# Reordered first loads and transposes in a squared-ReLU MLP kernel on one core

## The chip, the core and the metric

The kernel runs on one core of a Trainium2 chip. The metric is the time of one execution on the device in microseconds (us). TensorE (PE) does the matrix products and writes them to PSUM; VectorE (DVE) and ScalarE (ACT) move and transform data; GpSimd (POOL) and SyncE (SP) do little here but start transfers. DMA queues that SP, ACT and POOL issue to bring the inputs from HBM into SBUF.

## What is computed

`x` has 2048 rows of 576 numbers, `w1` is 576 x 4608, `w2` is 4608 x 576, all bf16:

```python
h = jnp.einsum("bsd,df->bsf", x, w1) + b1
r = jnp.where(h > zero, h, zero)
h = r * r
out = jnp.einsum("bsf,fd->bsd", h, w2) + b2
```

## The kernel before, in words

The 2048 rows are cut into four blocks of 512. A product with `w1` contracts over the 576 columns of `x`, so `x` must lie transposed in SBUF (`xTw`, one block per buffer, columns in windows of 128 partitions). For blocks 1 to 3 a transposing DMA does that (`load_xT`, L122). For block 0 it would come late, so PE does it: `x` is loaded as it is in four pieces of 128 rows (`x_sb`, `load_x` L71), and `x_transpose(j, k)` (L145) multiplies the 128 x 128 piece of row group j and column chunk k with an identity into a PSUM tile `tb`. I write T(j,k) for it. Chunks 0 to 3 are the first 512 columns; the fifth (k = NK) is the last 128, which overlap chunk 3 by half. Row groups 0 and 1 make half 0 of the block, 2 and 3 half 1. `x_copies(h)` (L151) then brings half h into `xTw` with five copies of 128 x 256: chunks 0, 2 and the fifth on DVE, 1 and 3 on ACT. Each of chunks 0 to 3 has a PSUM bank of its own for each half; the fifth shares the bank of chunk 2, in slot 1.

The 4608 columns of `w1` are 36 tiles of 128. The first four (`w1n`, and `w1n8` for the last 64 rows of the contraction) are the head of block 0: `a_full(0, "k_outer")` (L195) computes them while the rest of `w1` (`w1_h`) is still being loaded. Its unit is `part(h, k)` (L224): four matmuls of 256 columns, one per tile, that add chunk k of half h. The last 64 rows are added by `pair` (L202), four matmuls on 64 rows each that run two at a time. `dup_windows(0)` (L117) makes two big DVE copies within `xTw`, so that 64-row pieces lie in both halves of the partitions. `make_b1T` (L164) transposes the bias rows on PE into one bias per partition. After the head, `a_rows(0)` (L179) does the other 32 tiles with pairs of 64-row matmuls, and `evac_h` (L174) applies bias and ReLU on ACT and squares on DVE. The rest (`phase_t` and `phase_b`, the product with `w2`, and the three other blocks) follows on PE without a pause, in an order written out at L309 to L329.

The order of the head on PE before the change is: seven warm-up matmuls on constants (L61 to L63); T(0,0..3), T(1,0..3), the two fifth chunks, the copies of half 0; part(0,0); T(2,..); part(0,1), part(0,2); T(3,..), the copies of half 1, `dup_windows`; part(0,3), part(1,0), the bias transpose, part(1,1) to part(1,3), the pairs.

`keep` holds the instructions of each engine in the order of the program; the framework puts in the semaphore waits. It also gives every DMA that SP or ACT issues one of eight semaphores in turn, so that the ninth waits until the first has landed. SP issues x0, w1n0, w1n1, x3, w1n2, w1n3, then the first two pieces of `w1_h`, the two of `w1n8`, and the rest of `w1_h`; ACT issues x1 and x2; POOL issues `b1_rows` (36 rows of 256 B) and `b2_col` (L98, L100).

Of the kernel before, what the change touches and what calls it, by code (L numbers as in the profile page):

```python
# [11 lines left out]
BF16 = mybir.dt.bfloat16  # L12
FP32 = mybir.dt.float32
# [4 lines left out]
def kernel(  # L18
# [9 lines left out]
    nc = tc.nc  # L28
    keep = tc.keep_in_program_order
    P = 128  # L30
    H = 64
    x2 = x.flatten_outer_dims()
    out2 = out.flatten_outer_dims()
    S, D = x2.shape
    F = w1.shape[1]
    NFT = F // P
    NC = D // H
    NK = NC // 2
    G = 4
    GW = G * P  # L40
# [6 lines left out]
    DM = D - DT  # L47

    const = ctx.enter_context(tc.tile_pool(name="const", bufs=1))
    wpool = ctx.enter_context(tc.tile_pool(name="wpool", bufs=1))  # L50
# [5 lines left out]
    ps_h = ctx.enter_context(tc.tile_pool(name="ps_h", bufs=4, space=PSUM))  # L56
    ps_o = ctx.enter_context(tc.tile_pool(name="ps_o", bufs=4, space=PSUM))

    wps = ps_o.tile([P, 512], FP32, name="wps", tag="po")
    ones = nc.const_aps.tensor(1.0, [P, 512], BF16)  # L60
    WARM = [512] * 6 + [128]  # L61
    for i, n in enumerate(WARM):
        keep(nc.tensor.matmul(wps[:, 0:n], lhsT=ones[:, 0:P], rhs=ones[:, 0:n], start=True, stop=True))  # L63

    xs = const.tile([P, RT, D], BF16, name="x_sb")
    w1n = wpool.tile([P, NK, GW], BF16, name="w1n")
    w1n8 = wpool.tile([P, G // 2, P], BF16, name="w1n8")
    w1_h = wpool.tile([P, NC, FH], BF16, name="w1_h")
    w1_v = w1.rearrange("(c p) f -> p c f", p=H)

    def load_x(eng, rt):  # L71
        keep(eng.dma_start(out=xs[:, rt, :], in_=x2[rt * P:(rt + 1) * P, :]))

    def load_w1n(eng, k):
        keep(eng.dma_start(out=w1n[:, k, :], in_=w1[k * P:(k + 1) * P, 0:GW]))

    def load_w1n8(eng, h):
        src = w1[NK * P:D, 0:GW].rearrange("p (i h f) -> p i h f", h=2, f=P)
        keep(eng.dma_start(out=w1n8[h * H:(h + 1) * H, :, :], in_=src[:, :, h, :]))

    def load_w1(eng, h, j0, j1):
        keep(eng.dma_start(out=w1_h[h * H:(h + 1) * H, :, j0 * P:j1 * P],
                      in_=w1_v[:, :, GW + h * FH + j0 * P:GW + h * FH + j1 * P]))

    load_x(nc.sync, 0)
    load_x(nc.scalar, 1)
    load_w1n(nc.sync, 0)
    load_x(nc.scalar, 2)
    load_w1n(nc.sync, 1)
    load_x(nc.sync, 3)  # L90
    for k in range(2, NK):
        load_w1n(nc.sync, k)

    ident = const.tile([P, P], BF16, name="ident")
    make_identity(nc, ident[:])
    b1_rows = const.tile([P, P], BF16, name="b1_rows")
    nc.gpsimd.memset(b1_rows[:], 0.0)
    nc.gpsimd.dma_start(out=b1_rows[0:NFT, :], in_=b1.rearrange("(ft p) -> ft p", p=P))  # L98
    b2_col = const.tile([P, 1], BF16, name="b2_col")
    nc.gpsimd.dma_start(out=b2_col[:], in_=b2[DM:D].rearrange("(d o) -> d o", o=1))  # L100
    b2T = const.tile([P, 1], FP32, name="b2T")
    nc.gpsimd.tensor_copy(out=b2T[:], in_=b2_col[:])
    warm = const.tile([P, 1], FP32, name="warm")
    keep(nc.scalar.activation(out=warm[:], in_=nc.const_aps.tensor(0.0, [P, 1], FP32), func=ACT.Relu))

    E3, O, SPC, E = 0, 1, 5, 6
    LO_W = [O, O + 1, O + 2, O + 3, E, E + 1, E + 2, E3, SPC]
# [20 lines left out]

    w2_sb = wpool.tile([P, NFT, D], BF16, name="w2_sb")
    w2_view = w2.rearrange("(ft p) d -> p ft d", p=P)  # L130
    W2CH = 9

    def load_w2(c):
        keep(nc.sync.dma_start(out=w2_sb[:, c * W2CH:(c + 1) * W2CH, :], in_=w2_view[:, c * W2CH:(c + 1) * W2CH, :]))

# [2 lines left out]
    alloc_xT(0)  # L138
    xT0 = xT_blk[0]
    HS = SB // 2  # L140
    tb_po = [ps_o.tile([P, 2, HS], BF16, name="tb", tag="po") for _ in range(2)]
    tb_ph = [ps_h.tile([P, 2, HS], BF16, name="tb", tag="ph") for _ in range(4)]
    half_banks = [tb_ph, None]

    def x_transpose(j, k):  # L145
        h, q = divmod(j, 2)
        qc = slice(q * P, (q + 1) * P)
        bank, slot, c0 = (half_banks[h][k], 0, k * P) if k < NK else (half_banks[h][2], 1, D - P)
        keep(nc.tensor.transpose(bank[:, slot, qc], xs[:, j, c0:c0 + P], ident[:]))  # L149

    def x_copies(h):  # L151
        hc = slice(h * HS, (h + 1) * HS)
        for k in range(NK):
            src = half_banks[h][k][:, 0, :]
            if k % 2 == 0:
                keep(nc.vector.tensor_copy(out=xT0[:, O + k, hc], in_=src))  # L156
            else:
                keep(nc.scalar.copy(out=xT0[:, O + k, hc], in_=src))  # L158
        keep(nc.vector.tensor_copy(out=xT0[:, E3, hc], in_=half_banks[h][2][:, 1, :]))


    b1T = const.tile([P, NFT], FP32, name="b1T")

    def make_b1T():  # L164
        b1T_ps = ps_o.tile([P, P], BF16, name="b1T_ps", tag="po")
        keep(nc.tensor.transpose(b1T_ps[:], b1_rows[:], ident[:]))  # L166
        keep(nc.vector.tensor_copy(out=b1T[:], in_=b1T_ps[:, 0:NFT]))

# [26 lines left out]
    def a_full(sb, order):  # L195
        xT = xT_blk[sb]
        banks = []
        for g in range(G):
            pool, tag = (ps_o, "po") if g < 2 else (ps_h, "ph")
            banks.append(pool.tile([P, SB], FP32, name="pn", tag=tag))  # L200

        def pair(i, start, stop):  # L202
            keep(nc.tensor.matmul(banks[2 * i][:], lhsT=w1n8[0:H, i, :], rhs=xT[0:H, SPC, :],  # L203
                             start=start, stop=stop, skip_group_check=order == "k_outer"))
            keep(nc.tensor.matmul(banks[2 * i + 1][:], lhsT=w1n8[H:P, i, :], rhs=xT[H:P, E3, :],  # L205
                             start=start, stop=stop, skip_group_check=order == "k_outer"))

        def full(g, k, start, stop):
            keep(nc.tensor.matmul(banks[g][:], lhsT=w1n[:, k, g * P:(g + 1) * P], rhs=xT[:, O + k, :],  # L209
                             start=start, stop=stop))  # L210

        if order == "rows_first":
            for i in (1, 0):
                pair(i, True, False)
            for g in (2, 3, 0, 1):
                for k in range(NK):
                    full(g, k, False, k == NK - 1)
                evac_h(sb, banks[g], g)
        else:
            if order == "k_outer":  # L220
                tb_new = [ps_h.tile([P, 2, HS], BF16, name="tb", tag="ph") for _ in range(2)]
                half_banks[1] = tb_new + tb_po

                def part(h, k):  # L224
                    hc = slice(h * HS, (h + 1) * HS)
                    for g in range(G):
                        keep(nc.tensor.matmul(banks[g][:, hc], lhsT=w1n[:, k, g * P:(g + 1) * P],  # L227
                                              rhs=xT[:, O + k, hc], start=(h == 0 and k == 0), stop=False,
                                              skip_group_check=True))

                for j in range(2):
                    for k in range(NK):
                        x_transpose(j, k)
                for j in range(2):
                    x_transpose(j, NK)
                x_copies(0)
                part(0, 0)
                for k in range(NK + 1):
                    x_transpose(2, k)
                part(0, 1)  # L240
                part(0, 2)
                for k in range(NK + 1):
                    x_transpose(3, k)
                x_copies(1)
                dup_windows(0)
                part(0, 3)
                part(1, 0)
                make_b1T()
                for k in range(1, NK):
                    part(1, k)  # L250
            else:
                for g in (2, 3, 0, 1):
                    for k in range(NK):
                        full(g, k, k == 0, False)
            for i in (1, 0):
                pair(i, False, True)
                evac_h(sb, banks[2 * i], 2 * i)
                evac_h(sb, banks[2 * i + 1], 2 * i + 1)
# [35 lines left out]
    for (j0, j1) in [(0, 1), (1, 2), (2, 4), (4, 6), (6, 8), (8, 10), (10, 12)]:  # L294
        load_w1(nc.sync, 0, j0, j1)
        load_w1(nc.sync, 1, j0, j1)
        if j0 == 0:
            load_w1n8(nc.sync, 0)
            load_w1n8(nc.sync, 1)
    load_xT(1)  # L300
    for (j0, j1) in [(12, 14), (14, 16)]:
        load_w1(nc.sync, 0, j0, j1)
        load_w1(nc.sync, 1, j0, j1)
    keep(nc.sync.dma_start(out=b2_bc[:], in_=b2.partition_broadcast(P)))
    for c in (0, 2, 1, 3):
        load_w2(c)
    load_xT(2)

# [51 lines left out]
```

## Time and profile before

| | us |
|---|---|
| median of 5 runs | 290.97 (290.82 to 291.11) |
| the profiled execution, whole | 291.4 |
| its span, first to last instruction | 289.6 |
| PE busy | 285.6 (99%) |
| ACT busy | 96.7 (33%) |
| DVE busy | 78.5 (27%) |
| first transpose of x on PE begins | 3.65 |
| first `pair` on PE begins | 9.87 |

The profile lists instructions by the line of the program, with the engine, the tile that is written and those that are read, and the shape. In its timeline each row has the start and the length of a group in us, and in brackets how long the engine had been idle before it and what released it. A matmul's record reaches from its start to its modelled end and overlaps the next; the pace of PE is read from start to start. The profiled execution has its own time; a step is measured in it and then set against the median.

### The profile page before, as it was taken

How to read it: one execution, taken by the hardware profiler on the slowest of the kernel's cores; microseconds unless marked ns; L12 is line 12 of the kernel's file. 1: busy time of each engine (PE TensorE's matmuls, PEld its weight loads, DVE VectorE, ACT ScalarE, POOL GpSimd, SP SyncE). 2: the span in 40 equal slices, each digit the busy share in tenths (PEclk: the TensorE clock that was granted, in tenths of full speed). 3: DMA queues.
4: the chain of work that ended last, by engine and by line, in shares of the span. 5: the costliest groups of instructions: out<-in, count | busy, mean ns of one | idle time of the engine just before them, and what ended most of it. 6: DMA issues, size and time to landing. Idle time of an engine off the chain costs nothing.

```text
span 289.6 us, 4693 instructions
## 1 busy us (share of the span) xinstructions
PE 285.6 (99%) x2027; PEld 140.0 (48%) x2032; DVE 78.5 (27%) x176; ACT 96.7 (33%) x154; POOL 2.2 (1%) x10
## 2 busy tenths in 40 slices
PE   8999999999999999999999999999999999999996
PEld 5544444444444555555544444444444455555555
DVE  1644554444500200000015444444440001100001
ACT  2566666666500000000027666666670000000000
POOL 3000000000000000000000000000000000000000
PEclk9999999999999999999999999999999999999999
DMA  6999999800001200000000000000000110000100
GB/s 199 207 239 183 261 389 263 112 0 2 0 13 25 52 16 18 16 16 18 16 16 2 1 2 0 2 0 2 0 2 0 36 38 16 16 16 19 33 16 18
DMA packets 31605, 16.52 MB, mean 57 GB/s; under 512 B 15700, under 2 KB 31584, under 8 KB 31584
## 3 DMA queue, kind: packets, MB, share of 16 engines
q1 hardware_dynamic: 31232, 15.91, 23.0%
q8 instruction: 16, 0.26, 0.4%
q10 hardware_dynamic: 288, 0.30, 0.3%
q14 instruction: 5, 0.04, 0.0%
q0 software_dynamic: 64, 0.01, 0.0%
HBM read 11.36 MB, written 2.36 MB: 47 GB/s over the span
## 4 chain that ended last, share of the span: by engine, by line
PE 98%; DMA 1%; issue 0%; DVE 0%
PE ph L188 42%; PE po L289 38%; PE pt L270 11%; PE pn L209 4%; PE pn L227 1%; DMA x_sb<-in_x_dram 1%; PE tb L149 1%; PE ph L190 1%; PE pn L203 1%; DVE o_sb L291 0%; PE b1T_ps L166 0%; PE pn L205 0%
## 5 line engine op out<-in xcount | busy, mean ns | idle before, releaser
L188 PE MATMUL ph<-xTw,w_h 64*128 64x512 bf16 x576 | 124.6, 376 | 0.0
L190 PE MATMUL ph<-xTw,w_h 64*128 64x512 bf16 x576 | 124.6, 376 | 0.0
L289 PE MATMUL po<-w_sb,hT 128*128 128x448 bf16 (+2 forms) x612 | 109.4, 341 | 0.0
L176 ACT ACTIVATE r<-ph,b1T 128x512 bf16<-128x512 f32 x128 | 81.1, 685 | 41.6 <-PE ph L190 41.6
L188 PEld LDWEIGHTS <-w_h 64*128 64x128 bf16 x576 | 54.1, 94 | 68.3
L289 PEld LDWEIGHTS <-hT 128*128 128x128 bf16 x612 | 58.5, 98 | 51.0
L177 DVE TENSOR_TENSOR hT<-r 128x512 bf16<-128x512 bf16 x144 | 61.2, 426 | 75.9 <-ACT r L176 75.5
L190 PEld LDWEIGHTS <-w_h 64*128 64x128 bf16 x576 | 54.1, 94 | 0.0
L291 DVE TENSOR_TENSOR o_sb<-po,b_bc 128x448 bf16<-128x448 f32 (+2 forms) x17 | 10.2, 597 | 125.8 <-PE po L289 125.8
L270 PE MATMUL pt<-hT,w_sb 128*128 128x512 bf16 x142 | 31.3, 379 | 0.1
L176 ACT ACTIVATE r<-pn,b1T 128x512 bf16<-128x512 f32 x16 | 10.3, 688 | 61.0 <-PE pn L205 59.6
L270 PEld LDWEIGHTS <-w_sb 128*128 128x128 bf16 x144 | 14.1, 98 | 17.0
L273 ACT ACTIVATE oT<-pt,b2T 128x512 bf16<-128x512 f32 x4 | 2.8, 688 | 28.3 <-PE pt L270 28.3
L209 PE MATMUL pn<-xTw,w1n 128*128 128x512 bf16 x45 | 10.4, 379 | 0.4 <-issue 0.3
L209 PEld LDWEIGHTS <-w1n 128*128 128x128 bf16 x48 | 4.5, 98 | 6.0 <-issue 0.8
L227 PE MATMUL pn<-xTw,w1n 128*128 128x256 bf16 x32 | 4.8, 302 | 0.0
L227 PEld LDWEIGHTS <-w1n 128*128 128x128 bf16 x32 | 3.4, 109 | 0.5
L63 PE MATMUL wps<-const-bfloat16-1.0 128*128 128x512 bf16 (+1 forms) x7 | 2.8, 579 | 0.8 <-PEq L344 0.8
L156 DVE COPY xTw<-tb 128x256 bf16<-128x256 bf16 x4 | 1.1, 292 | 6.7 <-PE tb L149 6.7
L119 DVE COPY xTw<-xTw 64x2048 bf16<-64x2048 bf16 x4 | 2.8, 689 | 0.2
L120 DVE COPY xTw<-xTw 64x2048 bf16<-64x2048 bf16 x4 | 2.7, 687 | 0.1
L158 ACT COPY xTw<-tb 128x256 bf16<-128x256 bf16 x4 | 1.3, 375 | 3.8 <-PE tb L149 3.8
(23 smaller groups left out, 16.3 us busy)
## 6 DMA issues: line engine op xcount, KB each, us to landing
w_sb<-in_w_dram SPq DMA_DIRECT2D x4, 1296.0 KB, 13.0
w_h<-in_w_dram SPq DMA_DIRECT2D x14, 288.0 KB, 5.7
out_dram<-o_sb SPq DMA_DIRECT2D x15, 112.0 KB, 1.7
w_h<-in_w_dram SPq DMA_DIRECT2D x4, 144.0 KB, 3.3
w1n<-in_w_dram SPq DMA_DIRECT2D x4, 128.0 KB, 3.6
out_dram<-ot SPq DMA_DIRECT2D x4, 128.0 KB, 2.0
x_sb<-in_x_dram SPq DMA_DIRECT2D x2, 144.0 KB, 3.3
x_sb<-in_x_dram ACTq DMA_DIRECT2D x2, 144.0 KB, 3.3
```

The costliest lines, as they stand in the source:

```text
L63: keep(nc.tensor.matmul(wps[:, 0:n], lhsT=ones[:, 0:P], rhs=ones[:, 0:n], start=True, stop=True))
L149: keep(nc.tensor.transpose(bank[:, slot, qc], xs[:, j, c0:c0 + P], ident[:]))
L176: keep(nc.scalar.activation(out=r[:], in_=bank[:], func=ACT.Relu, bias=b1T[:, ft:ft + 1], scale=1.0))
L177: keep(nc.vector.tensor_tensor(out=hTs[sb][:, ft, :], in0=r[:], in1=r[:], op=ALU.mult))
L188: keep(nc.tensor.matmul(bx[:], lhsT=w1_h[0:H, LO_C[i], jc], rhs=xT[0:H, LO_W[i], :], start=(i == 0), stop=(i == NC - 1)))
L190: keep(nc.tensor.matmul(by[:], lhsT=w1_h[H:P, UP_C[i], jc], rhs=xT[H:P, UP_W[i], :], start=(i == 0), stop=(i == NC - 1)))
L203: keep(nc.tensor.matmul(banks[2 * i][:], lhsT=w1n8[0:H, i, :], rhs=xT[0:H, SPC, :], start=start, stop=stop, skip_group_check=order == "k_o ...
L209: keep(nc.tensor.matmul(banks[g][:], lhsT=w1n[:, k, g * P:(g + 1) * P], rhs=xT[:, O + k, :], start=start, stop=stop))
L227: keep(nc.tensor.matmul(banks[g][:, hc], lhsT=w1n[:, k, g * P:(g + 1) * P], rhs=xT[:, O + k, hc], start=(h == 0 and k == 0), stop=False, s ...
L270: keep(nc.tensor.matmul(pt[:], lhsT=w2_sb[:, ft, DM:D], rhs=hT[:, ft, :], start=(i == 0), stop=(i == NFT - 1)))
L289: keep(nc.tensor.matmul(po[:, 0:d1 - d0], lhsT=hT[:, ft, jj * P:(jj + 1) * P], rhs=w2_sb[:, ft, d0:d1], start=(i == 0), stop=(i == NFT - 1)))
L291: keep(nc.vector.tensor_tensor(out=o_sb[:, d0:d1], in0=po[:, 0:d1 - d0], in1=b2_bc[:, d0:d1], op=ALU.add))
```

## The change

- The loads on SP become x0, w1n0, w1n1, w1n2, the two of `w1n8`, then `w1_h`; those on ACT x1, x2, x3, w1n3, and, behind the ACT warm-up activation, `b1_rows`. POOL issues none. `b2_col` is loaded on SP ahead of `b2_bc`.
- `w1n8` holds all 512 columns in both halves of the partitions (twice the bytes, in runs of 1 KB).
- The transposes use four PSUM tiles `tb[h][bank]` with four slots each: chunks 0, 1 and the fifth of half h in slots 0, 1 and 2 of bank 0, chunks 2 and 3 in slots 0 and 1 of bank 1. The copy of a chunk is issued directly after the transpose that completes it. All copies are on DVE, except those of bank 1 of half 1, on ACT.
- The order on PE: T(0,..), T(1,..), part(0,0), T(2,..), part(0,1), T(3,..), part(0,2), part(0,3), part(1,0), bias transpose, part(1,1) to part(1,3), pairs.
- The last warm-up matmul has 256 columns in place of 128. The four accumulators of the head lie in one PSUM pool, and the warm-up and bias tiles in the other.
- `w2` is loaded in two pieces in place of four.

```diff
-    WARM = [512] * 6 + [128]
+    WARM = [512] * 6 + [256]
...
     load_x(nc.sync, 0)
     load_x(nc.scalar, 1)
-    load_w1n(nc.sync, 0)
-    load_x(nc.scalar, 2)
-    load_w1n(nc.sync, 1)
-    load_x(nc.sync, 3)
-    for k in range(2, NK):
-        load_w1n(nc.sync, k)
+    for k in range(2):
+        load_w1n(nc.sync, k, k + 1)
+        load_x(nc.scalar, 2 + k)
+    load_w1n(nc.sync, 2, 3)
+    load_w1n(nc.scalar, 3, 4)
...
+    keep(nc.scalar.dma_start(out=b1_rows[0:NFT, :], in_=b1.rearrange("(ft p) -> ft p", p=P)))
+    for h in range(2):
+        load_w1n8(nc.sync, h)
...
-    tb_po = [ps_o.tile([P, 2, HS], BF16, name="tb", tag="po") for _ in range(2)]
-    tb_ph = [ps_h.tile([P, 2, HS], BF16, name="tb", tag="ph") for _ in range(4)]
+    tb = [[ps_h.tile([P, 4, HS], BF16, name="tb", tag="ph") for _ in range(2)] for _ in range(2)]
+    PLACE = [(0, 0), (0, 1), (1, 0), (1, 1), (0, 2)]
+    T_ORDER = [0, 1, 2, 3, NK]
...
+    def x_transpose(j):
         h, q = divmod(j, 2)
+        hc = slice(h * HS, (h + 1) * HS)
+        for k in T_ORDER:
+            bank, slot = PLACE[k]
+            c0 = k * P if k < NK else D - P
+            keep(nc.tensor.transpose(tb[h][bank][:, slot, q * P:(q + 1) * P], xs[:, j, c0:c0 + P], ident[:]))
+            if q == 1:
+                w = O + k if k < NK else E3
+                if h == 1 and bank == 1:
+                    keep(nc.scalar.copy(out=xT0[:, w, hc], in_=tb[h][bank][:, slot, :]))
+                else:
+                    keep(nc.vector.tensor_copy(out=xT0[:, w, hc], in_=tb[h][bank][:, slot, :]))
...
                 for j in range(2):
-                    for k in range(NK):
-                        x_transpose(j, k)
-                for j in range(2):
-                    x_transpose(j, NK)
-                x_copies(0)
-                part(0, 0)
-                for k in range(NK + 1):
-                    x_transpose(2, k)
-                part(0, 1)
-                part(0, 2)
-                for k in range(NK + 1):
-                    x_transpose(3, k)
-                x_copies(1)
+                    x_transpose(j)
+                for k in range(2):
+                    part(0, k)
+                    x_transpose(2 + k)
                 dup_windows(0)
-                part(0, 3)
+                for k in range(2, NK):
+                    part(0, k)
                 part(1, 0)
                 make_b1T()
```

More of the change, by code (lines that the diff above doesn't have):

```diff
@@ L57 @@
     ps_o = ctx.enter_context(tc.tile_pool(name="ps_o", bufs=4, space=PSUM))
-    wps = ps_o.tile([P, 512], FP32, name="wps", tag="po")
+    wps = ps_h.tile([P, 512], FP32, name="wps", tag="ph")
     ones = nc.const_aps.tensor(1.0, [P, 512], BF16)
-    WARM = [512] * 6 + [128]
+    WARM = [512] * 6 + [256]
     for i, n in enumerate(WARM):
@@ L66 @@
     w1n = wpool.tile([P, NK, GW], BF16, name="w1n")
-    w1n8 = wpool.tile([P, G // 2, P], BF16, name="w1n8")
+    w1n8 = wpool.tile([P, GW], BF16, name="w1n8")
     w1_h = wpool.tile([P, NC, FH], BF16, name="w1_h")
@@ L72, in load_x, with load_w1n @@
         keep(eng.dma_start(out=xs[:, rt, :], in_=x2[rt * P:(rt + 1) * P, :]))
-    def load_w1n(eng, k):
-        keep(eng.dma_start(out=w1n[:, k, :], in_=w1[k * P:(k + 1) * P, 0:GW]))
+    def load_w1n(eng, k0, k1):
+        src = w1[k0 * P:k1 * P, 0:GW].rearrange("(k p) f -> p k f", p=P)
+        keep(eng.dma_start(out=w1n[:, k0:k1, :], in_=src))
     def load_w1n8(eng, h):
-        src = w1[NK * P:D, 0:GW].rearrange("p (i h f) -> p i h f", h=2, f=P)
-        keep(eng.dma_start(out=w1n8[h * H:(h + 1) * H, :, :], in_=src[:, :, h, :]))
+        keep(eng.dma_start(out=w1n8[h * H:(h + 1) * H, :], in_=w1[NK * P:D, 0:GW]))
     def load_w1(eng, h, j0, j1):
@@ L83, in load_w1 @@
                       in_=w1_v[:, :, GW + h * FH + j0 * P:GW + h * FH + j1 * P]))
+    b1_rows = const.tile([P, P], BF16, name="b1_rows")
+    nc.vector.memset(b1_rows[:], 0.0)
     load_x(nc.sync, 0)
     load_x(nc.scalar, 1)
-    load_w1n(nc.sync, 0)
-    load_x(nc.scalar, 2)
-    load_w1n(nc.sync, 1)
-    load_x(nc.sync, 3)
-    for k in range(2, NK):
-        load_w1n(nc.sync, k)
+    for k in range(2):
[3 more added lines that the diff above has]
+    load_w1n(nc.scalar, 3, 4)
     ident = const.tile([P, P], BF16, name="ident")
     make_identity(nc, ident[:])
[L96 to L102, printed above, removed]
     warm = const.tile([P, 1], FP32, name="warm")
     keep(nc.scalar.activation(out=warm[:], in_=nc.const_aps.tensor(0.0, [P, 1], FP32), func=ACT.Relu))
+    keep(nc.scalar.dma_start(out=b1_rows[0:NFT, :], in_=b1.rearrange("(ft p) -> ft p", p=P)))
+    for h in range(2):
+        load_w1n8(nc.sync, h)
     E3, O, SPC, E = 0, 1, 5, 6
@@ L130 @@
     w2_view = w2.rearrange("(ft p) d -> p ft d", p=P)
-    W2CH = 9
+    W2CH = 18
     def load_w2(c):
@@ L140 @@
     HS = SB // 2
-    tb_po = [ps_o.tile([P, 2, HS], BF16, name="tb", tag="po") for _ in range(2)]
-    tb_ph = [ps_h.tile([P, 2, HS], BF16, name="tb", tag="ph") for _ in range(4)]
-    half_banks = [tb_ph, None]
-    def x_transpose(j, k):
+    tb = [[ps_h.tile([P, 4, HS], BF16, name="tb", tag="ph") for _ in range(2)] for _ in range(2)]
+    PLACE = [(0, 0), (0, 1), (1, 0), (1, 1), (0, 2)]
+    T_ORDER = [0, 1, 2, 3, NK]
+    def x_transpose(j):
         h, q = divmod(j, 2)
[L147 to L151, printed above, removed]
         hc = slice(h * HS, (h + 1) * HS)
-        for k in range(NK):
[L154 to L159, printed above, removed]
+        for k in T_ORDER:
[8 more added lines that the diff above has]
+                    keep(nc.vector.tensor_copy(out=xT0[:, w, hc], in_=tb[h][bank][:, slot, :]))
     b1T = const.tile([P, NFT], FP32, name="b1T")
     def make_b1T():
-        b1T_ps = ps_o.tile([P, P], BF16, name="b1T_ps", tag="po")
+        b1T_ps = ps_h.tile([P, P], BF16, name="b1T_ps", tag="ph")
         keep(nc.tensor.transpose(b1T_ps[:], b1_rows[:], ident[:]))
@@ L198, in a_full @@
         for g in range(G):
-            pool, tag = (ps_o, "po") if g < 2 else (ps_h, "ph")
+            pool, tag = (ps_o, "po") if g < 2 or order == "k_outer" else (ps_h, "ph")
             banks.append(pool.tile([P, SB], FP32, name="pn", tag=tag))
         def pair(i, start, stop):
-            keep(nc.tensor.matmul(banks[2 * i][:], lhsT=w1n8[0:H, i, :], rhs=xT[0:H, SPC, :],
+            keep(nc.tensor.matmul(banks[2 * i][:], lhsT=w1n8[0:H, 2 * i * P:(2 * i + 1) * P], rhs=xT[0:H, SPC, :],
                              start=start, stop=stop, skip_group_check=order == "k_outer"))
-            keep(nc.tensor.matmul(banks[2 * i + 1][:], lhsT=w1n8[H:P, i, :], rhs=xT[H:P, E3, :],
+            keep(nc.tensor.matmul(banks[2 * i + 1][:], lhsT=w1n8[H:P, (2 * i + 1) * P:(2 * i + 2) * P], rhs=xT[H:P, E3, :],
                              start=start, stop=stop, skip_group_check=order == "k_outer"))
@@ L220, in a_full @@
             if order == "k_outer":
-                tb_new = [ps_h.tile([P, 2, HS], BF16, name="tb", tag="ph") for _ in range(2)]
-                half_banks[1] = tb_new + tb_po
                 def part(h, k):
@@ L231, in a_full @@
                 for j in range(2):
-                    for k in range(NK):
-                        x_transpose(j, k)
-                for j in range(2):
-                    x_transpose(j, NK)
-                x_copies(0)
-                part(0, 0)
-                for k in range(NK + 1):
-                    x_transpose(2, k)
-                part(0, 1)
-                part(0, 2)
-                for k in range(NK + 1):
-                    x_transpose(3, k)
-                x_copies(1)
+                    x_transpose(j)
+                for k in range(2):
+                    part(0, k)
+                    x_transpose(2 + k)
                 dup_windows(0)
-                part(0, 3)
+                for k in range(2, NK):
+                    part(0, k)
                 part(1, 0)
@@ L296 @@
         load_w1(nc.sync, 1, j0, j1)
-        if j0 == 0:
-            load_w1n8(nc.sync, 0)
-            load_w1n8(nc.sync, 1)
     load_xT(1)
@@ L303 @@
         load_w1(nc.sync, 1, j0, j1)
+    b2_col = const.tile([P, 1], BF16, name="b2_col")
+    keep(nc.sync.dma_start(out=b2_col[:], in_=b2[DM:D].rearrange("(d o) -> d o", o=1)))
+    b2T = const.tile([P, 1], FP32, name="b2T")
+    nc.gpsimd.tensor_copy(out=b2T[:], in_=b2_col[:])
     keep(nc.sync.dma_start(out=b2_bc[:], in_=b2.partition_broadcast(P)))
-    for c in (0, 2, 1, 3):
+    for c in range(2):
         load_w2(c)
```

## The prediction

> **What bounds the kernel now.** I read the page first, then the chain of work that ended last, then the timeline of PE and of DVE over the first 12 us. The page:
>
> ```profile
> PE 285.6 (99%) x2027; PEld 140.0 (48%) x2032; DVE 78.5 (27%) x176; ACT 96.7 (33%) x154; POOL 2.2 (1%) x10
> ...
> PE 98%; DMA 1%; issue 0%; DVE 0%
> ```
>
> PE is the bound from end to end; only 1% of the chain is a transfer, and that is x0, which lands at 3.60. What PE does after the head isn't touched, so the change is worth what it moves the first `pair`, at 9.87. The timeline of PE:
>
> ```profile
> 0.78 2.83 PE L63 MATMUL wps<-const-bfloat16-1.0 128*128 128x512 bf16 x7 [0.78 <-PEq L344]
> 3.65 1.25 PE L149 MATMUL tb<-ident,x_sb 128*128 128x128 bf16 x10
> 4.75 1.01 PE L227 MATMUL pn<-xTw,w1n 128*128 128x256 bf16 x4
> 5.55 0.74 PE L149 MATMUL tb<-ident,x_sb 128*128 128x128 bf16 x5
> 6.08 1.34 PE L227 MATMUL pn<-xTw,w1n 128*128 128x256 bf16 x8
> 7.26 0.44 PE L149 MATMUL tb<-ident,x_sb 128*128 128x128 bf16 x5
> 7.54 1.04 PE L227 MATMUL pn<-xTw,w1n 128*128 128x256 bf16 x8
> 8.41 0.22 PE L166 MATMUL b1T_ps<-ident,b_rows 128*128 128x128 bf16 x1
> 8.47 1.47 PE L227 MATMUL pn<-xTw,w1n 128*128 128x256 bf16 x12
> 9.87 0.39 PE L203 MATMUL pn<-xTw,w1n 64*128 64x512 bf16 x1
> ```
>
> Two things are to be seen. First, between 3.65 and 9.87 PE hardly waits: every group starts where the one before has started its last matmul. The only lost time is 0.055 ahead of 4.75 and 0.095 ahead of 9.87, which comes back at each change from 128 to 64 rows (150.04 has it too). Second, PE has two paces. Five transposes take 0.74 at 5.55 and 0.44 at 7.26; less the last one's record (0.31 and 0.22) that is 0.107 and 0.056 from start to start. A 256-column matmul takes 0.213 early and 0.109 late (the twelve of 8.47). The pace doubles at about 6.7, inside the eight of 6.08. So an idle 0.1 us before 6.7 costs 0.05, and a later change of pace costs half its delay.
>
> The timeline of DVE:
>
> ```profile
> 4.40 0.29 DVE L156 COPY xTw<-tb 128x256 bf16<-128x256 bf16 x1 [4.40 <-PE tb L149]
> 4.94 0.29 DVE L156 COPY xTw<-tb 128x256 bf16<-128x256 bf16 x1 [0.24 <-PE tb L149]
> 5.14 0.28 DVE L159 COPY xTw<-tb 128x256 bf16<-128x256 bf16 x1
> 7.51 0.52 DVE L156 COPY xTw<-tb 128x256 bf16<-128x256 bf16 x2 [2.09 <-PE tb L149]
> ```
>
> The copy at 4.40 follows T(1,0), which started at 4.05: 0.35 from the start of a transpose to its copy. The row at 4.94 is the one that decides this case. It copies chunk 2, slot 0 of its bank. Its last transpose T(1,2) started at 4.26 and ended at 4.58, and DVE sat idle from 4.69; yet it was released by the end of T(1,NK) at 4.90, which writes slot 1 of the same bank. So the waits are kept for a whole PSUM bank, not for a slot. In this kernel that cost DVE 0.24 us and PE nothing.
>
> **The change part by part.**
>
> *Transposes and copies.* In the new order T(1,0) goes to bank 0 slot 0, then its copy is issued, then T(1,1) to slot 1 of the same bank. If waits are kept by bank, T(1,1) may not start until that copy has read. The same for T(1,3) behind the copy of chunk 2, and for T(3,1) and T(3,3) in half 1: four waits of PE, which serves in order, so all behind them wait too. One wait: 0.35 from transpose to copy, 0.29 for the copy, 0.05 from its end to PE (4.69 to 4.75), 0.70 at the slow pace in place of 0.107; at the fast pace 0.26 (7.26 to 7.51) + 0.29 + 0.05 = 0.60 in place of 0.056. Bounds: nothing, if slots are tracked apart; 0.70 each. I take 0.70, by the row at 4.94.
>
> [...]
>
> Step by step, at the slow pace: T(0,..) 3.65 to 4.16. T(1,0) 4.16, its copy 4.51 to 4.80, T(1,1) 4.85, T(1,2) 4.96. Copy 1 5.20 to 5.50; copy 2 follows 0.22 later (as 7.51 and 7.74), 5.43 to 5.72; T(1,3) 5.77, T(1,4) 5.88. part(0,0) 5.99 to 6.84; T(2,..) to 7.37; part(0,1) to 8.23. T(3,0) 8.23, T(3,1) 8.92, T(3,2) 9.03; its ACT copy (0.375 by the rows of L158) 9.38 to 9.75, T(3,3) 9.81, T(3,4) 9.91; part(0,2) 10.02.
>
> *The pace.* PE is now idle 0.59, 0.70, 0.59 and 0.67 in turn. When does the pace double? In the trace it doubled 3.04 after the end of the last pause longer than 0.06 (that of 0.25 before 3.65), and 5.9 after the first matmul. Bounds: at 6.7 as before, or 5.9 after the last pause, 9.81 + 5.9 = 15.7. I take the nearest row, 3.04 after the last pause: 12.85. From 10.02: part(0,2), (0,3), (1,0) are 3 x 0.853 to 12.58, the bias transpose to 12.69, 0.16 of part(1,1) to 12.85; its other 0.69 at half the time, 0.35, to 13.20; two parts at 0.436 to 14.08; 0.095 for the change of rows: first `pair` at 14.17. Against 9.87 that is **+4.30**.
>
> [...]
>
> *Loads.* x0 and x1 keep their places, so 3.65 stands. x3 is issued at about 1.67 on ACT instead of 2.14, w1n3 at about 2.15 instead of 3.09; w1n1 and x3 now run side by side. By the landings of before (w1n1 5.61, x3 5.80, w1n3 6.68) nothing comes later than about 6.7, and PE asks for w1n1 at 7.37, x3 at 8.23, w1n2 at 10.02. Gain: 0, as PE didn't wait for them before either. `w1n8` and `w1_h` go through the ring of eight semaphores on SP: `w1n8` waits for landings at 3.6 to 4.6, the first two of `w1_h` leave at about 5.2 and 5.9 instead of 3.8 and 4.6 and land by about 9; they were needed at 10.3, now at 14.6. Cover 1 us even in the old timing. Later ones keep their turn.
>
> *Bias.* `b1_rows` leaves ACT behind four issues of 0.45 and the table load (1.28) at about 4.1. POOL's took 3.7 to land, which makes 7.8; asked for at 12.6, or 8.4 in the old timing. Cost 0; without that cover, PE would wait in order. `b2_col` at about 28 us is needed at 84. ACT is free when its two copies come.
>
> *The rest.* The longer warm-up matmul (0.107 more) fits into the pause of 0.25 before 3.65: 0, or down to -0.05 if it mattered. The `w2` pieces landed at 39 to 49 and are first read at 76.5; merging them moves none by 27 us. `dup_windows` follows at 10.6 to 12.0, before the pairs.
>
> Sum: 289.6 + 4.3 = 293.9 of span, 291.4 + 4.3 = 295.7 for the profiled execution; the runs' median lies 0.4 below that execution, so 290.97 + 4.3 = **295.3**.
>
> **The rivals.** (a) The same waits, but the pace doubles at 6.7 as before. The first two waits then cost half and the last two 0.54 each more than a fast transpose; run through the same steps, `pair` comes at 11.70: +1.83, 292.8. For it: matmuls still fill more than half of the time before 6.7. Against: PE worked from 0.78 to 3.40 without a pause, and that alone didn't double the pace. (b) The pace doubles as soon as the last pause is over, at 9.81, because two thirds of the time before it were work: part(0,2) at 9.92, `pair` at 12.69, +2.82, 293.8. (c) The not-slower side: PE's write after a read is tracked by slot, and only a read after a write by bank. Then no wait arises; T(1,0) is the sixth transpose rather than the fifth, so part(0,0) waits for its copy till 4.85, and the sum is +0.05: 291.0. It decides if T(1,1) starts 0.107 after T(1,0). For it: no row shows PE waiting for another slot's copy, since before never asked it. Against: the row at 4.94. (d) The pace doubles at the far bound, 15.7: half of the 2.85 more, +5.73, 296.7.
>
> **How the numbers follow.** Forecast 0.60; (a) 0.15; (b) 0.12; (c) 0.07, of which a gain above 0.2% is 0.02; (d) 0.06. A measurement of this kernel tells about 0.2%, 0.6 us, from no change. The range runs from (a), less 0.3, to the forecast and 0.7: half of a doubling 1.0 later, and 0.2 for the lengths of the four waits. That is 292.5 to 296.0. It leaves out (c) and (d), 0.13. Faster 0.02, same 0.05, slower 0.93.
>
> **What would show it.** Right: T(1,1) starts 0.7 after T(1,0) with the DVE copy ending just before; four such breaks in the groups of transposes; 256-column matmuls 0.213 apart until about 13; first `pair` near 14.2; nothing different from there on. Wrong: ten transposes in one row; or four breaks with a fast pace before 10; or a wait of PE on `b1_rows`, `w1n` or `w1_h`.

## The result, and the profile after

The changed kernel is slower. The median of 21 runs is 292.50 us (292.17 to 295.78), against 290.99 for 40 runs of the kernel before. The ratio 1.0084 (95% interval 1.0065 to 1.0102) compares means, 293.48 and 291.05; the medians alone give 1.0052. The forecast was 295.3 with a range of 292.5 to 296.0, so the direction held, but the likeliest case was not the usual one, and the median lies on the lower end of the range by luck: ten of the 21 runs are below 292.5. The times are not spread evenly. Of the 21 runs 13 lie at 292.2 to 292.6, two at 293.8 to 293.9 and six at 295.6 to 295.8. The profiled execution took 292.17 with a span of 290.4, so it shows the first of these groups.

The timeline of PE in the changed kernel, up to the first `pair`:

```profile
0.77 2.93 PE L63 MATMUL wps<-const-bfloat16-1.0 128*128 128x512 bf16 x7 [0.77 <-PEq L328]
3.54 0.51 PE L148 MATMUL tb<-ident,x_sb 128*128 128x128 bf16 x6
4.44 0.27 PE L148 MATMUL tb<-ident,x_sb 128*128 128x128 bf16 x2 [0.38 <-DVE xTw L154]
5.23 0.27 PE L148 MATMUL tb<-ident,x_sb 128*128 128x128 bf16 x2 [0.52 <-DVE xTw L154]
5.34 0.60 PE L218 MATMUL pn<-xTw,w1n 128*128 128x256 bf16 x4
5.78 0.44 PE L148 MATMUL tb<-ident,x_sb 128*128 128x128 bf16 x5
6.06 0.60 PE L218 MATMUL pn<-xTw,w1n 128*128 128x256 bf16 x4
6.50 0.22 PE L148 MATMUL tb<-ident,x_sb 128*128 128x128 bf16 x1
7.10 0.27 PE L148 MATMUL tb<-ident,x_sb 128*128 128x128 bf16 x2 [0.38 <-DVE xTw L154]
7.83 0.27 PE L148 MATMUL tb<-ident,x_sb 128*128 128x128 bf16 x2 [0.46 <-ACT xTw L152]
7.94 1.47 PE L218 MATMUL pn<-xTw,w1n 128*128 128x256 bf16 x12
9.25 0.22 PE L160 MATMUL b1T_ps<-ident,b_rows 128*128 128x128 bf16 x1
9.30 1.47 PE L218 MATMUL pn<-xTw,w1n 128*128 128x256 bf16 x12
10.71 0.39 PE L197 MATMUL pn<-xTw,w1n 64*128 64x512 bf16 x1
```

Where before had ten transposes in one row, the rows now break at T(1,1), T(1,3), T(3,1) and T(3,3), and the brackets name the copy that ended each wait: three on DVE, one on ACT. The bracket counts from the modelled end of the last matmul; from start to start the breaks are 0.60, 0.74, 0.60 and 0.68 where a transpose at this pace takes 0.056, so 2.40 us are lost. The chain of work that ended last (start, length, what) goes through the same copies, none of which stood in it before:

```profile
4.09 0.30 DVE xTw L154
4.40 0.04 issue
4.44 0.23 PE tb L148
4.67 0.02 issue
4.69 0.50 DVE xTw L154 x2
...
6.75 0.30 DVE xTw L154
...
7.41 0.38 ACT xTw L152
```

But the first `pair` comes at 10.71 and not 2.40 later than 9.87. The second row of the timeline says why: six transposes from 3.54 take 0.51, less 0.22 for the last record 0.058 each. PE has its double pace from the first transpose, while in the profiled execution of before it got it at about 6.7. Between 3.65 and 6.69 before did 2.99 us of work at the single pace; at the double pace that takes about 1.5. So the sum of this pair of executions is 2.40 for the waits, -1.5 for the pace, -0.11 since x0 landed earlier, -0.06 for the wait ahead of part(0,0) that before had: about +0.75; `pair` moved by 0.84 and the span by 0.8. From `pair` to the end both take about 279.7.

### The profile page after: what moved, and what is told of

The parts are those of the page before. It is cut to its first block, busy times and chain, and to the rows that moved or that the text cites. A ratio compares the mean times of both kernels' runs of the same rounds, so it can differ in the third digit from the quotient of the medians.

```text
span 290.4 us, 4691 instructions
## 1 busy us (share of the span) xinstructions
PE 284.7 (98%) x2027; PEld 139.0 (48%) x2032; DVE 79.3 (27%) x179; ACT 96.2 (33%) x152; POOL 0.9 (0%) x7
## 4 chain that ended last, share of the span: by engine, by line
PE 98%; DVE 0%; issue 0%; ACT 0%
PE ph L182 42%; PE po L272 38%; PE pt L253 11%; PE pn L203 4%; PE pn L218 1%; PE wps L63 1%; PE ph L184 1%; PE pn L197 1%; PE tb L148 1%; DVE xTw L154 0%; ACT xTw L152 0%; DVE o_sb L274 0%; PE b1T_ps L160 0%; PE pn L199 0%
## 5 line engine op out<-in xcount | busy, mean ns | idle before, releaser
L218 PE MATMUL pn<-xTw,w1n 128*128 128x256 bf16 x32 | 4.0, 273 | 0.0
L148 PE MATMUL tb<-ident,x_sb 128*128 128x128 bf16 x20 | 2.3, 219 | 1.7 <-DVE xTw L154 1.3
L154 DVE COPY xTw<-tb 128x256 bf16<-128x256 bf16 x8 | 2.1, 289 | 5.4 <-PE tb L148 5.4
L116 DVE COPY xTw<-xTw 64x2048 bf16<-64x2048 bf16 x4 | 2.8, 689 | 0.2
L148 PEld LDWEIGHTS <-x_sb 128*128 128x128 bf16 x20 | 1.4, 98 | 2.8 <-issue 2.2
```

The costliest lines, as they stand in the source:

```text
L148: keep(nc.tensor.transpose(tb[h][bank][:, slot, q * P:(q + 1) * P], xs[:, j, c0:c0 + P], ident[:]))
```

## The experiments

Theory W: PE waits four times for a copy out of the PSUM bank that it is to write next, and these pauses may also hold back its pace. Rival L: the new loads and the ACT queue cost the time. All ratios are against the kernel before on the same chip.

**loads_only and transposes_only** cut the change in two. The first has the loads, queues and bias of the change, with everything of the transposes as before; the second is the reverse.

```diff
 # loads_only, against the changed kernel
-                for j in range(2):
-                    x_transpose(j)
-                for k in range(2):
-                    part(0, k)
-                    x_transpose(2 + k)
+                for j in range(2):
+                    for k in range(NK):
+                        x_transpose(j, k)
...
+                x_copies(0)
+                part(0, 0)
```

> The changed kernel with the transposes, copies, PSUM tiles, warm-up and PE order of before: only the loads, the queues and the bias are those of the change. Theory W (four waits of PE for copies out of the same PSUM bank, and the pace of PE behind them): 291.0, as before, all runs between 290.4 and 291.8, none near 293.8 or 295.7. Rival L (the new loads and the ACT queue cost the time): 292.5.

> The kernel before with only the transposes, copies, PSUM tiles, warm-up and PE order of the change; all loads as before. Theory W: as the changed kernel, most runs at 292.2 to 292.6 and some at 295.7. Rival L: 291.0.

Measured: loads_only 291.22 (290.89 to 291.79), ratio 1.0004 (0.9995 to 1.0013). transposes_only 293.34, ratio 1.0097 (1.0059 to 1.0135); its six runs lie at 292.5 (two), 292.7, 294.0 and 295.85 (two). L falls; the whole loss, with its groups, belongs to the transposes and copies.

**copies_late** takes away what makes PE wait: the same tiles and slots, but the copies of a half stand behind all its transposes.

```diff
             keep(nc.tensor.transpose(tb[h][bank][:, slot, q * P:(q + 1) * P], xs[:, j, c0:c0 + P], ident[:]))
-            if q == 1:
+        if q == 1:
+            for k in T_ORDER:
+                bank, slot = PLACE[k]
                 w = O + k if k < NK else E3
```

> The changed kernel, but the five copies of a half are issued behind all its transposes, so that no transpose follows a copy out of its bank. Theory W: the four waits go; part(0,0) waits once for its copy, about 0.5 at the fast pace, against 2.4 for the four: 292.4 - 1.9 = 290.5 to 291.5, with no group of runs at 293.8 or 295.7. Rival L: 292.5, groups as in the changed kernel.

Measured: 291.13 (290.62 to 291.63), ratio 1.0005 (0.9996 to 1.0013), no run above 291.7. The timeline of PE in copies_late:

```profile
3.53 1.25 PE L148 MATMUL tb<-ident,x_sb 128*128 128x128 bf16 x10
5.16 0.65 PE L220 MATMUL pn<-xTw,w1n 128*128 128x256 bf16 x4 [0.38 <-DVE xTw L156]
5.65 0.44 PE L148 MATMUL tb<-ident,x_sb 128*128 128x128 bf16 x5
5.93 0.60 PE L220 MATMUL pn<-xTw,w1n 128*128 128x256 bf16 x4
6.37 0.44 PE L148 MATMUL tb<-ident,x_sb 128*128 128x128 bf16 x5
```

Ten transposes in one row again, five and five behind; one wait is left, that of part(0,0) for the first copy. So the moment when a copy is issued accounts for the whole loss, within the noise.

**half1_late** does this for half 1 alone and leaves the two waits of half 0.

```diff
-            if q == 1:
...
+            if j == 1:
+                x_copy(h, k)
+        if j == 3:
+            for k in T_ORDER:
+                x_copy(h, k)
```

> The changed kernel with the copies of half 1 alone issued behind its transposes: two of the four waits, those of T(3,1) and T(3,3), go. Theory W: 0.55 + 0.62 at the fast pace, 292.4 - 1.2 = 291.2 for most runs, and the late group comes sooner, no run above 294. If the waits counted only through the pace: 292.4 still. Rival (only the first half matters): 292.4.

Measured: seven of 12 runs at 291.0 to 291.9, five at 292.9 to 293.5, median 291.72, ratio 1.0042 (1.0022 to 1.0061). Both groups stand below those of the changed kernel: the lower by about 1.1, close to the price of two waits at the double pace (0.55 + 0.62), the upper by about 2.5. No run lies above 294, as expected.

**fill and fill_again** leave the waits and take away the idleness: matmuls on constants stand ahead of T(1,1) and T(1,3), written to an accumulator that part(0,0) starts anew, so the output is the same.

```diff
+            if fill is not None and k in (1, 3):
+                for n in (512, 128):
+                    keep(nc.tensor.matmul(fill[:, 0:n], lhsT=ones[:, 0:P], rhs=ones[:, 0:n], start=True, stop=True))
...
-                for j in range(2):
-                    x_transpose(j)
+                x_transpose(0)
+                x_transpose(1, banks[0])
```

> The changed kernel with matmuls on constants (512 and 128 columns, 0.53 at the slow pace, 0.27 at the fast) ahead of T(1,1) and of T(1,3), written to an accumulator that is started anew later: PE works while it would wait. Theory W with a pace that is raised by an unbroken stretch of work: the four waits stay, most runs at 292.4 as in the changed kernel, but the groups at 293.8 and 295.7 vanish. Rival (the groups have another cause, a late transfer for instance): six of 21 runs stay near 295.7.

> The kernel fill once more, for more runs, beside the changed kernel on the same chip. Theory W with the pace: again no run above 293.5, median 292.5. Rival: runs near 295.7, as often as in the changed kernel beside it.

**after_again** is the changed kernel once more, beside fill_again.

> The changed kernel itself, beside fill_again. Groups at 292.4 and 295.7, about one run in three in the upper one; if the profiled execution falls there, its 256-column matmuls are 0.213 apart until about 13 (theory W with the pace), or fast before 7 (rival: another cause).

Measured: fill 292.51 (292.45 to 292.88), fill_again 292.51 (292.44 to 292.68), five runs each and none above 292.9. after_again: 292.2, 292.5, 293.9, and three at 295.6 to 295.7. With the first 21 runs and transposes_only, 15 of 33 runs with bare waits lie above 293.5, and none of 10 with filled ones. The timeline of PE in fill:

```profile
3.50 0.84 PE L151 MATMUL tb<-ident,x_sb 128*128 128x128 bf16 x6
4.14 0.58 PE L150 MATMUL pn<-const-bfloat16-1.0 128*128 128x512 bf16 x2
4.72 0.27 PE L151 MATMUL tb<-ident,x_sb 128*128 128x128 bf16 x2
4.83 0.43 PE L150 MATMUL pn<-const-bfloat16-1.0 128*128 128x512 bf16 x2
5.52 0.27 PE L151 MATMUL tb<-ident,x_sb 128*128 128x128 bf16 x2 [0.25 <-DVE xTw L157]
```

The transposes T(1,1) and T(1,3) come at 4.72 and 5.52, hardly earlier than in the profile of after_again (4.72 and 5.57); work without use in between removes the upper groups. Runs held up by a late transfer would not go away by that. Runs held up by PE's pace, if pauses keep it low, would, and no_warm below shows such a pace in a trace (0.213 for a matmul of 256 columns). The profile of after_again is of a run at 292.51, so no trace of the changed kernel itself in the upper group exists.

**no_warm** makes such a trace certain: the changed kernel without the warm-up matmuls.

```diff
-    WARM = [512] * 6 + [256]
-    for i, n in enumerate(WARM):
-        keep(nc.tensor.matmul(wps[:, 0:n], lhsT=ones[:, 0:P], rhs=ones[:, 0:n], start=True, stop=True))
```

> The changed kernel without its seven warm-up matmuls, so that PE begins with T(0,0) at 3.5 and has no stretch of work without a long pause before 9.8. Theory W with a pace that is raised by an unbroken stretch of work: the pace doubles in every run only between about 12.6 and 16, all runs at 295 to 297, and the profile shows 256-column matmuls 0.213 apart up to there. If the group near 295.7 came from something else: 292.4 plus at most half of the 2.8 of lost warm-up, below 294.

Measured: four runs at 295.25 to 296.19, ratio 1.0158 (1.0143 to 1.0174). Its timeline of PE:

```profile
3.39 0.82 PE L144 MATMUL tb<-ident,x_sb 128*128 128x128 bf16 x6 [3.39 <-DMA x_sb<-in_x_dram]
4.59 0.37 PE L144 MATMUL tb<-ident,x_sb 128*128 128x128 bf16 x2 [0.38 <-DVE xTw L150]
5.43 0.37 PE L144 MATMUL tb<-ident,x_sb 128*128 128x128 bf16 x2 [0.47 <-DVE xTw L150]
5.60 1.06 PE L214 MATMUL pn<-xTw,w1n 128*128 128x256 bf16 x4
6.46 0.74 PE L144 MATMUL tb<-ident,x_sb 128*128 128x128 bf16 x5
...
9.53 2.77 PE L214 MATMUL pn<-xTw,w1n 128*128 128x256 bf16 x12
12.09 0.31 PE L156 MATMUL b1T_ps<-ident,b_rows 128*128 128x128 bf16 x1
12.20 2.61 PE L214 MATMUL pn<-xTw,w1n 128*128 128x256 bf16 x12
14.74 0.39 PE L193 MATMUL pn<-xTw,w1n 64*128 64x512 bf16 x1
```

Twelve matmuls of 256 columns take 2.77 at 9.53, 0.213 from start to start; the changed kernel took 1.47 for the same twelve. The pace doubles only at the end of the row of 12.20, at about 14.5, 5 us after the last pause. Up to there this is the step-by-step list of the forecast, 0.3 to 0.4 early: T(1,1) 4.59, T(1,3) 5.43, T(3,1) 8.54, T(3,3) 9.37.

**own_bank and own_bank_old_loads** try for a version that beats both: chunk 0 of each half alone in its bank, so that its copy lies beside eight transposes in half 0 and four in half 1, and all other copies late; the second with the loads of before.

```diff
-    PLACE = [(0, 0), (0, 1), (1, 0), (1, 1), (0, 2)]
+    PLACE = [(0, 0), (1, 0), (1, 1), (1, 2), (1, 3)]
...
                 for j in range(2):
-                    x_transpose(j)
+                    x_transpose(j, [0])
+                x_copy(0, [0])
+                for j in range(2):
+                    x_transpose(j, T_ORDER[1:])
+                x_copy(0, T_ORDER[1:])
```

> The changed kernel with chunk 0 of each half alone in bank 0 and the four others in bank 1; of half 0, T(0,0) and T(1,0) come first, then the copy of chunk 0, then the eight others, then their copies; so no transpose follows a copy out of its bank, and the first copy lies beside eight transposes. Theory W: as copies_late less its one wait of about 0.5: 290.4 to 290.9, the fastest. Rival (the loads give the floor): 291.1.

> The kernel own_bank with the loads, queues, bias and w2 pieces of before. In own_bank PE waited 0.28 for x3 (landed 6.35) and the median was that of copies_late. If the new loads hold it back: 290.6 to 290.9. If any order of the first loads is the floor: 291.0 to 291.3.

Measured: own_bank 291.27 (290.74 to 291.70), ratio 1.0009 (1.0000 to 1.0017), and not the fastest; own_bank_old_loads 290.90, ratio 0.9995 (0.9987 to 1.0004). The timeline of PE in own_bank:

```profile
3.51 1.31 PE L147 MATMUL tb<-ident,x_sb 128*128 128x128 bf16 x10
4.61 0.92 PE L218 MATMUL pn<-xTw,w1n 128*128 128x256 bf16 x4
5.37 0.44 PE L147 MATMUL tb<-ident,x_sb 128*128 128x128 bf16 x5
5.68 0.61 PE L218 MATMUL pn<-xTw,w1n 128*128 128x256 bf16 x4
6.40 0.45 PE L147 MATMUL tb<-ident,x_sb 128*128 128x128 bf16 x5
```

No wait for a copy is left: part(0,0) starts as the tenth transpose gives way. Yet the fifth row starts 0.27 late: x3 landed at 6.35, so in this execution a PE that is ready sooner runs into the loads. Nothing here beats the kernel before by more than its noise. The 290.90 of own_bank_old_loads is the upper end of what was expected if the new loads hold PE back, but the two load orders differ by 0.1% with intervals that overlap, so that is not shown.

**loads_bias_sp** follows up a wait that loads_only showed on PE. Its ACT timeline, then its PE timeline:

```profile
4.39 0.79 ACTq L99 DMA_DIRECT2D b_rows<-in_b_dram  x1
5.22 0.65 ACT L155 COPY xTw<-tb 128x256 bf16<-128x256 bf16 x2 [1.11 <-DVE xTw L156]
```

```profile
4.49 0.49 PE L224 MATMUL pn<-xTw,w1n 128*128 128x256 bf16 x3
5.64 0.27 PE L224 MATMUL pn<-xTw,w1n 128*128 128x256 bf16 x1 [0.67 <-ACT xTw L155]
```

The issue of the bias DMA holds ACT's queue from 4.39 to 5.18, the copies of chunks 1 and 3 start behind it, and PE, whose fourth accumulator lies in chunk 1's bank, waits for them. In the changed kernel half 0 has no copy on ACT, and ACT's next work behind that DMA is the copy at 7.41. The edit, against loads_only:

```diff
-    keep(nc.scalar.dma_start(out=b1_rows[0:NFT, :], in_=b1.rearrange("(ft p) -> ft p", p=P)))
+    keep(nc.sync.dma_start(out=b1_rows[0:NFT, :], in_=b1.rearrange("(ft p) -> ft p", p=P)))
```

> The kernel loads_only with the bias rows issued on SP, behind the first loads and ahead of w1n8, instead of on ACT. In loads_only the ACT copy of chunk 1 began only at 5.22, behind the bias DMA, which waited in ACT's queue for an earlier landing (4.92), and PE waited 0.67 for it. Theory: that wait goes, and the time falls by 0.1 to 0.5, to 290.7 to 291.1. Rival (PE would wait for w1n1 there anyway): 291.2.

Measured: 291.31, ratio 1.0007 (0.9998 to 1.0016), no gain. The expectation failed. The 4.92 that it calls a landing is, in the trace of loads_only, the end of a DVE copy; no transfer is complete at that moment, and why the issue took 0.79, where it took 0.59 in the changed kernel, stays open. In the trace of loads_bias_sp both waits are gone, ACT first and then PE:

```profile
4.28 0.65 ACT L155 COPY xTw<-tb 128x256 bf16<-128x256 bf16 x2
```

```profile
4.52 1.01 PE L224 MATMUL pn<-xTw,w1n 128*128 128x256 bf16 x4
```

But that execution still had the single pace in this row (1.01 for four, as at 4.75 in the profile of before; loads_only has 0.49 for three at 4.49), so the two traces don't compare; why the median doesn't move stays open.

**before_warm256** lengthens the last warm-up matmul of the kernel before, and nothing else.

```diff
-    WARM = [512] * 6 + [128]
+    WARM = [512] * 6 + [256]
```

> The kernel before with the last warm-up matmul of 256 columns in place of 128 and nothing else. Theory W: it lies in the pause before x0 lands, 291.0 as before, within 0.1. If the pause before the first transpose kept the pace low: 290.5.

Measured: 290.85, ratio 0.9999 (0.9989 to 1.0008): no effect. Its profile serves as a match for that of after_again. Rows of PE in before_warm256, then in after_again:

```profile
3.50 1.27 PE L149 MATMUL tb<-ident,x_sb 128*128 128x128 bf16 x10
...
5.43 0.45 PE L149 MATMUL tb<-ident,x_sb 128*128 128x128 bf16 x5
...
9.36 0.39 PE L203 MATMUL pn<-xTw,w1n 64*128 64x512 bf16 x1
```

```profile
3.50 0.84 PE L148 MATMUL tb<-ident,x_sb 128*128 128x128 bf16 x6
4.72 0.37 PE L148 MATMUL tb<-ident,x_sb 128*128 128x128 bf16 x2 [0.38 <-DVE xTw L154]
5.57 0.27 PE L148 MATMUL tb<-ident,x_sb 128*128 128x128 bf16 x2 [0.47 <-DVE xTw L154]
...
11.04 0.39 PE L197 MATMUL pn<-xTw,w1n 64*128 64x512 bf16 x1
```

In the first the pace doubled at about 5.4, just ahead of the row in which five transposes take 0.45; in the second at about 5.2, between the rows in which two transposes take 0.37 and 0.27. The first transpose starts at 3.50 in both. The first `pair` comes 1.68 later, and the two executions took 290.88 and 292.51, +1.63. This, and not the 0.8 of the first pair of profiles, is the price in the lowest group, where most runs lie: the medians differ by 1.51.

## Why the prediction was right or wrong

- *PE bounds, and only the head counts*: right. From the first `pair` on nothing differs (about 279.7 in both).
- *Four waits, from the one row at 4.94*: right in number and place, and nearly in size. Forecast for one wait 0.70 at the single and 0.60 at the double pace; measured 0.69 to 0.79 (no_warm) and 0.60 to 0.74 (the changed kernel). copies_late shows that they are the cause and half1_late that they add up.
- *The pace doubles at 12.85, 3.04 after the last pause*: this step failed as the likeliest case. It took when the pace doubled in one trace for a property of the kernel. It is one of the execution: in two profiles of the changed kernel it came before 3.6 and at about 5.2, in others that keep the warm-up by 4.0 (loads_only, where four transposes from there take 0.39), before 4.8 (fill and half1_late), at about 5.4 (before_warm256) and at about 6.7 (before), and in no_warm at about 14.5. Where it comes by about 5.2, the pauses don't hold it back, and the change costs some 1.5. Otherwise the times fit a PE that stays at the single pace beyond 9.8, as forecast; a trace shows that for no_warm alone, and there the pace doubled 5.1 after the last pause and not 3.04. The sum for that case, 295.3, lies 0.3 to 0.6 below the group at 295.6 to 295.85, 11 of 33 runs; rival (a), 292.8, lies 0.1 to 0.6 above the group of 18 that sets the median. Rival (b), 293.8, lies at the middle group, 293.8 to 294.0 (4 of 33), but no trace fell into it, so its cause stays open; no run came near the 296.7 of rival (d). So the likeliest case of the forecast fits a third of the runs, where it was given 0.60.
- *The five runs of before*: their spread of 0.3 made the moment of doubling look fixed. With 40 runs they spread over 1.35, from 290.44 to 291.79.
- *What sets the moment of doubling*: no run shows it. In after_again the pace was single in the row of 4.72 and double in that of 5.57, with a pause of 0.47 between them; in no_warm, where the pauses were as long (0.38 to 0.47 in the brackets), it doubled only at about 14.5. As the moment differs so from one execution to another, the groups should have been forecast with weights: of the runs with bare waits 15 of 33 lie above 293.5. Why the upper group is as narrow as it is, 11 runs within 0.23, was not shown either.
- *Loads, bias, warm-up cost 0*: right (loads_only, before_warm256). The bias rows were asked for at 9.25 without a wait. That `w2` in two pieces costs nothing is within loads_only. Not foreseen: the bias DMA can hold ACT for later work, as loads_only shows (0.79 for its issue, and 0.67 of waiting on PE).
- *Rival (c)*, waits by slot: refuted by the four brackets. In all these kernels the slots of one bank belong to one tile, so whether the waits are kept for the bank or for the tile was not tested.

## What to carry to other kernels

Ask of every pair of a PE write and a read by another engine whether they share a PSUM bank (here also a tile), not whether they share data: a copy put right behind its transpose made the next transpose into that bank wait for it, 0.6 to 0.8 us from start to start here. Either group the writes of a bank ahead of its reads (copies_late), or let the writes that follow a copy go to another bank (own_bank). Near the start of a kernel, a pause of PE cost more than its length in a part of these executions (11 of 33 runs took 4.6 to 4.8 more than the kernel before, where the four pauses themselves lost 2.40 in the profiled execution); so read several profiles, or a distribution of times, before taking the moment when PE's pace doubles for a constant.

## What the runs showed that was not expected

The moment when PE's pace doubles differs between executions of one program, by 1.6 us or more in two profiles of the changed kernel (before 3.6 and at about 5.2). Together with four pauses of 0.6 to 0.8 us this goes with three separate groups of times, 3.3 us apart from the lowest to the highest. A quarter to half a microsecond of useless matmuls inside each of two pauses removes the upper ones (0 of 10 runs against 15 of 33) at no cost to the median.
